# Split attention with a feed-forward network: the score matmuls' operands cut from 128 rows to a head's own 64

## The chip, the cores and the metric

The kernel runs on one core of a Trainium2 chip. The metric is the time of the device in microseconds (us). Two runs of the kernel before took 238.03 and 238.21 us, median 238.12.

The engines are named as the profile names them: PE is TensorE's matmul stream and PEld its weight loads (one operand of a matmul is first loaded into the array as weights, the other then streams through), DVE is VectorE, ACT ScalarE, POOL GpSimd, SP SyncE, which here only issues DMAs. L405 is line 405 of the kernel.

## The reference

Attention over 4 batches, 8 heads, 768 positions and 64 values per head. Heads 0, 2 and 6 see all earlier positions. The other five see the first 4 positions and the last 64. The eight heads' outputs stand side by side as 512 features of 3,072 tokens, which a two-layer network with a leaky rectifier takes from 512 to 2,048 and back to 512.

```python
scores = scale * np.matmul(q, k.transpose(0, 1, 3, 2))
stream_keep = causal & (is_sink | in_win)          # n_sink = 4, window = 64
mask = where(is_retrieval[h], causal, stream_keep)
a = softmax(where(mask, scores, -1e9))
x = (a @ v)  ->  [3072, 512]
h = x @ w_in
out = (max(h, 0) + alpha * min(h, 0)) @ w_out
```

## The kernel before

The work is cut into 16 segments (n = 0 to 15): four batches, and in each four pairs of heads, `PAIRS = [(0, 1), (2, 3), (6, 7), (4, 5)]`. `hh` (0 or 1) is a head's place in its pair. All matmuls take bf16 operands and add up in fp32 in PSUM, which is treated as eight banks of 512 columns.

**Queries and keys.** The score matmul contracts over the 64 values of a head, so queries and keys are needed with these values on the partitions. `qT[n % 4]` holds both heads of a segment one above the other: head 0 on rows 0 to 63, head 1 on rows 64 to 127. The keys have one array for each head, `kTs[n % 4][hh]`, of 128 rows: the head's own 64 rows (64 hh to 64 hh + 63) carry its keys and the other 64 rows are zeros, written at the start by the items kz0 to kz3. A score matmul over all 128 rows thus multiplies the other head's queries by zero. In segments 0 to 7 the transposes are done on TensorE (`to_array`, L342 to L348) and copied out by `put_q` (L353) and `put_k` (L368, L372 to L374). From segment 8 on DMAs transpose (`dma_q`, `dma_k`); the zeros then come along with the transposed rows, from a buffer zeroed by the items nz0 and nz1.

**Scores.** `S_retr` (a head that sees everything) and `S_stream` (a head with a window) write the scores with the keys on the partitions, 128 keys at a time: the keys are the weights and the queries stream. `S_retr` lays six blocks of keys one after another and cuts the whole into six parts of equal length, so that a matmul (L405) has anything from 16 to 488 columns. `S_stream` has 176 or 192 columns per block of keys, fewer at the end (L438 from segment 8 on, L444 before). In segments 0 to 3 a mask is added on TensorE, by a second matmul of the identity with a mask of large negative numbers into the same columns (L408, L447); from segment 4 on masked entries are instead multiplied by zero after the exponential, on VectorE (`M_retr`, `M_stream`). Each score item takes a bank of PSUM, or two before segment 4, which the exponential on ScalarE (L415, L463, L469) gives back.

**What follows.** `AV` (L501) multiplies the exponentials by the values, with a column of ones beside the values for the sums. `AV_out` (L510, L511) divides. The result is transposed to `xT`, on TensorE (L523, L528) or by DMA. `P1` (L543) is the first layer, `relu` and `prelu` (L548 on ScalarE, L555 on VectorE) the rectifier, `P2` (L563) the second layer, L569 and L573 the way out. The slopes alpha are transposed once on TensorE (L593). `warm` (L642) is a row of matmuls that uses nothing, ahead of the first transposes.

**Order.** Nothing is planned while building. `ORDER`, at the head of the file, names every item of work (S5.0.2 is score part 2 of head 0 in segment 5, s5.0.2 its exponential, m5.0.2 its mask, A, X, P and O as above), and the program issues the items in this order; each engine takes its own in that order. Feed-forward items of one batch are laid between score and attention items of the next. The last score matmuls start at 166.5 us; attention, transposes and feed-forward work follow. Instructions wait for each other by semaphores that follow from the tiles, rows and columns they read and write.

Of the kernel before, what the change touches and what calls it, by code (L numbers as in the profile page):

```python
# [73 lines left out]
def kernel(  # L74
# [14 lines left out]
    B, H, S, D = q.shape  # L89
# [31 lines left out]
    def tiles(n):  # L121
        return NEAR if n >= LAY else FAR
# [34 lines left out]
    NF, NK, NV, NR, NS = 4, 4, 5, 2, 3  # L157
# [11 lines left out]
    qT = [qT_all[:, i] for i in range(NK)]  # L169
    kTs = [[kT_all[:, i, h] for h in range(2)] for i in range(NK)]  # L170
# [213 lines left out]
    def score_bank(n, hh, m):  # L384
        held["S", n, hh, m] = got = take(*(SC2 if n < 4 else SC))
        return P[:, got[0]:got[0] + len(got), :]

    def r_parts(n, m):
        return range(2 * m, 2 * m + 2) if n < 4 else [m]

    def S_retr(n, hh, m):
        qt, kt = qT[n % NK], kTs[n % NK][hh]
        QS, RM, RO, RB = tiles(n).QS, tiles(n).RM, tiles(n).RO, tiles(n).RB
        sc = score_bank(n, hh, m)
        for x, part in enumerate(r_parts(n, m)):
            lo, hi = RB[part], RB[part + 1]
            for j in range(6):
                o, w = RO[j], S - QS[j]
                a, z = max(lo, o), min(hi, o + w)
                if a < z:  # L400
                    c = QS[j] + a - o

                    y = min(z, o + RM[j])
                    masked = n < 4 and a < y
                    nc.tensor.matmul(sc[:, x, a - lo:z - lo], kt[:, 128 * j:128 * (j + 1)],  # L405
                                     qt[:, c:c + z - a], start=True, stop=not masked)
                    if masked:
                        nc.tensor.matmul(sc[:, x, a - lo:y - lo], ident, nmr[:, max(j - 1, 0), a - o:y - o],  # L408
                                         start=False, stop=True)
# [19 lines left out]
    def thirds(n, m):  # L429
        return (range(0, 2), range(2, 3))[m] if n < 4 else range(m, m + 1)  # L430

    def S_stream(n, hh, m):
        qt, kt = qT[n % NK], kTs[n % NK][hh]
        sc = score_bank(n, hh, m)
        if n >= LAY:
            for x, j in enumerate(range(2 * m, NT if m == 2 else 2 * m + 2)):
                w = min(176, S - 112 * j)
                nc.tensor.matmul(sc[:, 0, 176 * x:176 * x + w], kt[:, 128 * j:128 * (j + 1)],  # L438
                                 qt[:, 112 * j:112 * j + w], start=True, stop=True)
            return  # L440
        for x, part in enumerate(thirds(n, m)):
            o = 0
            for j, w in THIRD[part]:
                nc.tensor.matmul(sc[:, x, o:o + w], kt[:, 128 * j:128 * (j + 1)],  # L444
                                 qt[:, 124 * j:124 * j + w], start=True, stop=n >= 4)
                if n < 4:
                    nc.tensor.matmul(sc[:, x, o:o + w], ident, (nms6 if j == 6 else nms)[:, 0:w],  # L447
                                     start=False, stop=True)
                o += w
# [247 lines left out]
    for n in range(NSEG):  # L697
# [21 lines left out]
        for hh, h in enumerate(heads(n)):  # L719
            k_ = (3 if n < 4 else 6) if RETR[h] else (2 if n < 4 else 3)  # L720
            for m in range(k_):
                item(f"S{n}.{hh}.{m}", S_retr if RETR[h] else S_stream, n, hh, m)
                item(f"s{n}.{hh}.{m}", E_retr if RETR[h] else E_stream, n, hh, m)
                if n >= 4:
                    item(f"m{n}.{hh}.{m}", M_retr if RETR[h] else M_stream, n, hh, m)
            item(f"A{n}.{hh}", AV, n, hh)
            item(f"a{n}.{hh}", AV_out, n, hh)
# [63 lines left out]
```

## Time and profile before

| | |
|---|---|
| median of the runs | 238.12 us |
| the profiled execution's own time | 237.75 us |
| its span, first to last instruction | 236.0 us |
| TensorE, matmuls (PE) | 226.6 us busy, 1,997 records |
| TensorE, weight loads (PEld) | 143.2 us busy, 2,026 records |
| VectorE | 160.2 us busy |
| ScalarE | 137.1 us busy |
| score matmuls L405, busy | 24.3 us, x132 |
| score matmuls before segment 8 of the heads with a window, L444, busy | 10.4 us, x70 |
| mean granted TensorE clock | 1.000 |

A line of the groups of instructions gives source line, engine, operation, the tile written and the tiles read, the shape and the count; after the bar the busy time in us and the mean length of one in ns. For matmuls the shape begins with the rows and columns of the array that are used (128*128), then partitions x columns of the moving operand. A line of the instructions in order of time gives start and length in us, then the same. In the page's slices each digit is the busy share of one fortieth of the span, in tenths. Matmuls are pipelined: the length of one reaches to the modelled end of its last column, and the next one starts well before that. The chain that ended last is followed back from the last instruction, at each step to what released it.

### The profile page before, as it was taken

To read this page: it belongs to the slowest core of one execution; us is meant where nothing else is said; L and a number is where in the kernel's file an instruction comes from. 1 tells how busy PE (TensorE), PEld (TensorE's weight loads), DVE (VectorE), ACT (ScalarE), POOL (GpSimd) and SP (SyncE) were. 2 spreads that over 40 slices of the span, in tenths; PEclk is the share of its full clock that TensorE was granted. 3 is DMA by queue.
4 is the path that set the end of the run, shared out by engine and by line. 5 is a ranking of instruction groups with operands and counts; after the bars stand their busy time and mean duration, and the time that the engine had idled before them with its cause. 6 is when DMAs were issued, how large, how long until landed. Compare 5 with 4: busy or idle time off the path is not lost.

```text
span 236.0 us, 5222 instructions
## 1 busy us (share of the span) xinstructions
PE 226.6 (96%) x1997; PEld 143.2 (61%) x2026; DVE 160.2 (68%) x404; ACT 137.1 (58%) x265; POOL 45.2 (19%) x92
## 2 busy tenths in 40 slices
PE   7889899999999999999999999999999999999994
PEld 6679555676666644676666455567755554565453
DVE  5879669997998766788994568967961057563020
ACT  6768349988674676785743567858312253650240
POOL 5775884000311800000010010000001010100000
PEclk9999999999999999999999999999999999999999
DMA  6999999998959999998989999961032020010123
GB/s 196 305 247 243 259 247 250 228 204 182 215 89 207 206 240 221 223 156 184 187 174 186 178 244 141 178 95 44 3 68 87 4 89 1 22 71 0 44 102 123
DMA packets 90529, 36.25 MB, mean 154 GB/s; under 512 B 77688, under 2 KB 88712, under 8 KB 90504
## 3 DMA queue, kind: packets, MB, share of 16 engines
q1 hardware_dynamic: 84520, 26.66, 58.4%
q0 software_dynamic: 5664, 8.91, 17.3%
q8 instruction: 16, 0.26, 0.5%
q10 hardware_dynamic: 320, 0.34, 0.4%
q14 instruction: 9, 0.07, 0.1%
HBM read 27.55 MB, written 6.29 MB: 143 GB/s over the span
## 4 chain that ended last, share of the span: by engine, by line
PE 81%; DMA 5%; SPq 4%; DVE 4%; issue 2%; ACT 2%; POOL 0%; POOLq 0%; DVEq 0%; ACTq 0%
PE P L543 33%; PE P L563 31%; PE P L501 6%; PE P L405 4%; DMA vf<-in_v_dram 3%; DMA alpha_r<-in_moe_alpha_dram 2%; PE P L438 2%; PE P L579 1%; SPq L232 1%; DVE g L555 1%; SPq L210 1%; SPq L234 1%; PE P L642 1%; PE P L523 1%; PE P L444 1%
## 5 line engine op out<-in xcount | busy, mean ns | idle before, releaser
L555 DVE SCALAR_TENSOR_TENSOR g<-neg,oma,P 128x256 bf16<-128x256 f32 (+1 forms) x128 | 72.7, 609 | 46.7 <-ACT neg L548 45.5
L543 PE MATMUL P<-xT,w_in_b 128*128 128x256 bf16 (+1 forms) x499 | 92.5, 324 | 0.7
L563 PE MATMUL P<-w_out_b,g 128*128 128x512 bf16 x352 | 86.4, 379 | 0.8
L548 ACT ACTIVATE neg<-P 128x512 f32<-128x512 f32 x96 | 55.0, 606 | 33.5 <-PE P L543 30.3
L543 PEld LDWEIGHTS <-w_in_b 128*128 128x128 bf16 x512 | 48.7, 98 | 29.2 <-issue 0.4
L563 PEld LDWEIGHTS <-g 128*128 128x128 bf16 x368 | 34.0, 98 | 33.4
L415 ACT ACTIVATE eR<-P 128x488 bf16<-128x488 f32 (+4 forms) x63 | 38.0, 624 | 19.2 <-PE P L405 16.6
L573 POOL DMA_DIRECT2D out_dram<-ot x18 | 10.3, 573 | 124.2 <-ACT ot L569 116.6
L569 ACT COPY ot<-P 128x512 f32<-128x512 f32 x23 | 13.2, 589 | 25.1 <-PE P L563 22.7
L405 PE MATMUL P<-qT,kT 128*128 128x280 bf16 (+16 forms) x132 | 24.3, 272 | 0.2
L511 DVE TENSOR_TENSOR xn<-P,rcp 128x448 bf16<-128x448 f32 x32 | 20.0, 624 | 1.1
L463 ACT ACTIVATE eS<-P 128x352 bf16<-128x352 f32 x30 | 14.1, 475 | 8.1 <-PE P L438 8.1
L469 ACT ACTIVATE eS<-P 128x384 bf16<-128x384 f32 (+1 forms) x25 | 13.5, 558 | 5.2 <-PE P L444 2.2
L405 PEld LDWEIGHTS <-kT 128*128 128x128 bf16 x132 | 11.2, 97 | 7.1 <-DVE kT L368 0.2
L501 PE MATMUL P<-vb,eR 128*128 128x65 bf16 x324 | 11.9, 193 | 0.4 <-ACT eR L415 0.3
L501 PEld LDWEIGHTS <-eR 128*128 128x128 bf16 x324 | 11.1, 97 | 1.9 <-ACT eR L415 0.4
L501 PEld LDWEIGHTS <-eS 128*128 128x128 bf16 x260 | 10.3, 97 | 3.0 <-DVE vb L278 0.5
L501 PE MATMUL P<-vb,eS 128*128 128x65 bf16 x260 | 11.1, 193 | 0.3 <-DVE vb L278 0.3
L444 PE MATMUL P<-qT,kT 128*128 128x192 bf16 (+2 forms) x70 | 10.4, 234 | 0.2 <-ACT eR L415 0.2
L478 DVE TENSOR_TENSOR eS<-eS,ms_near 128x352 bf16<-128x352 bf16 x30 | 9.7, 334 | 1.3 <-ACT eS L463 1.3
L333 POOL CAST vb<-vf 128x896 bf16<-128x896 f32 x6 | 5.6, 933 | 25.9 <-DMA vf<-in_v_dram 24.9
L372 DVE COPY kT<-P 64x744 bf16<-64x744 bf16 x9 | 8.4, 933 | 1.6 <-ACT kT L368 1.4
(98 smaller groups left out, 189.7 us busy)
## 6 DMA issues: line engine op xcount, KB each, us to landing
qf<-in_q_dram SPq DMA_DIRECT2D x15, 384.0 KB
out_dram<-ot POOLq DMA_DIRECT2D x18, 256.0 KB, 3.8
vf<-in_v_dram SPq DMA_DIRECT2D x22, 192.0 KB
kf<-in_k_dram SPq DMA_DIRECT2D x21, 192.0 KB
w_in_b<-in_moe_w_in_dram POOLq DMA_DIRECT2D x4, 512.0 KB, 9.6
w_out_b<-in_moe_w_out_dram POOLq DMA_DIRECT2D x4, 512.0 KB, 18.4
kf<-in_k_dram SPq DMA_DIRECT2D x9, 196.0 KB
vf<-in_v_dram SPq DMA_DIRECT2D x9, 196.0 KB
```

Of the source, the lines that this page charges most:

```text
L405: nc.tensor.matmul(sc[:, x, a - lo:z - lo], kt[:, 128 * j:128 * (j + 1)], qt[:, c:c + z - a], start=True, stop=not masked)
L415: nc.scalar.activation(ebuf[n, hh][:, lo:hi].rearrange("p (x c) -> p x c", x=len(parts)), P[:, got[0]:got[0] + len(parts), 0:(hi - lo) // ...
L444: nc.tensor.matmul(sc[:, x, o:o + w], kt[:, 128 * j:128 * (j + 1)], qt[:, 124 * j:124 * j + w], start=True, stop=n >= 4)
L463: nc.scalar.activation(slots, sc[:, 0:352].rearrange("p (s c) -> p s c", c=176), AF.Exp, scale=scale)
L469: nc.scalar.activation(slots, sc.rearrange("p x (s c) -> p x s c", c=192), AF.Exp, scale=scale)
L501: nc.tensor.matmul(pav[:, i, :], e[:, o:o + 128], vv[:, j, hh, 0:D + 1], start=(m == 0), stop=(m == len(terms) - 1))
L511: nc.vector.tensor_tensor(xn[n][:, :, 64 * hh:64 * hh + 64], pav[:, :, 0:D], rcp.to_broadcast([128, NT, D]), op=ALU.mult)
L543: nc.tensor.matmul(psg[:, w * i:w * (i + 1)], w_in_b[:, a, 128 * fb:128 * (fb + 1)], xT[:, c, o:o + w], start=(c == 0), stop=(c == 3))
L548: nc.scalar.activation(neg[t, f], bank(held["P", t, f][0]), AF.Relu, scale=-1.0)
L555: nc.vector.scalar_tensor_tensor(g_buf[t % 2][:, fb, 0:w], neg[t, f][:, c], oma[:, fb:fb + 1], bank(got[0])[:, c], op0=ALU.mult, op1=ALU.add)
L563: nc.tensor.matmul(bank(held["O", t, s][0]), g_buf[t % 2][:, f, 128 * s:128 * (s + 1)], w_out_b[:, f, :], start=(f == 0), stop=(f == 15))
L569: nc.scalar.copy(ot, bank(got[0]))
```

## The change

Both score functions take, of `qT` and of the head's own key array, the 64 rows of that head in place of all 128. For head 0 these are rows 0 to 63, for head 1 rows 64 to 127. The loops over parts and blocks, the columns, the banks and `ORDER` stay. The mask matmuls of segments 0 to 3 still use the identity over 128 rows. The zero rows are still written, though the score matmuls no longer read them.

```diff
     def S_retr(n, hh, m):
-        qt, kt = qT[n % NK], kTs[n % NK][hh]
+        own = slice(D * hh, D * hh + D)
+        qt, kt = qT[n % NK][own], kTs[n % NK][hh][own]
         QS, RM, RO, RB = tiles(n).QS, tiles(n).RM, tiles(n).RO, tiles(n).RB
         sc = score_bank(n, hh, m)
...
     def S_stream(n, hh, m):
-        qt, kt = qT[n % NK], kTs[n % NK][hh]
+        own = slice(D * hh, D * hh + D)
+        qt, kt = qT[n % NK][own], kTs[n % NK][hh][own]
         sc = score_bank(n, hh, m)
```

## The prediction

> **What bounds the kernel now.** I read the views from coarse to fine. First the page: busy times, slices and the shares of the chain that ended last.
>
> ```profile
> PE 226.6 (96%) x1997; PEld 143.2 (61%) x2026; DVE 160.2 (68%) x404; ACT 137.1 (58%) x265; POOL 45.2 (19%) x92
> ...
> PE   7889899999999999999999999999999999999994
> ...
> PEclk9999999999999999999999999999999999999999
> ...
> PE 81%; DMA 5%; SPq 4%; DVE 4%; issue 2%; ACT 2%; POOL 0%; POOLq 0%; DVEq 0%; ACTq 0%
> ```
>
> TensorE is busy in nine tenths of every slice after the first few, at full clock, and it is 81% of the chain. So a nanosecond put into or taken out of its stream moves the end by about as much, wherever no wait of TensorE swallows it.
>
> The busy row counts a matmul to its modelled end, and ends overlap the next start. I therefore go by starts. Two forms in the groups by shape give the rule: 128x65 takes 193 ns, 128x512 takes 379 ns; the slope is 186/447 = 0.416 ns per column, the fixed part 166 ns. In a stream, starts follow each other by the slope alone plus some 2 ns: the 25 attention matmuls from 13.26 us on come about 30 ns apart. Summed that way (columns x 0.416 + 2.4 ns over 1,997 records) TensorE streams 216 us of the 231 between its first and last start. The score matmuls stream 24.4 us of it, in 272 pieces: lines L405 (132), L444 (70), L438 (70).
>
> Then the instructions in order of time, TensorE and its weight loads, in a stretch where all matmuls have one shape of array (128*128):
>
> ```profile
> 6.02 0.35 PE L405 MATMUL P<-qT,kT 128*128 128x454 bf16 x1
> 6.21 0.22 PE L408 MATMUL P<-nmr,ident 128*128 128x128 bf16 x1
> ...
> 6.02 0.10 PEld L408 LDWEIGHTS <-ident 128*128 128x128 bf16 x1
> ```
>
> The weights of the mask matmul L408 load while the score matmul before it streams; 0.19 us after that one's start (454 columns) the next one starts. Nothing is drained.
>
> Last, the two places where the shape of the array changes in this kernel: the transposes of head 0 (L346, 64 columns) give way to full ones (L348), and the 16-row transpose of the slopes (L593) to the feed-forward (L543).
>
> ```profile
> 5.26 0.22 PE L346 MATMUL P<-ident,g 128*64 128x128 bf16 x1
> 5.40 0.11 PEld L348 LDWEIGHTS <-g 128*128 128x128 bf16 x2
> 5.41 0.23 PE L348 MATMUL P<-ident,g 128*128 128x128 bf16 x1
> ...
> 29.69 0.20 PE L593 MATMUL P<-ident_f,alpha_r 16*128 16x16 f32 x1 [1.25 <-DMA alpha_r<-in_moe_alpha_dram]
> 29.83 0.39 PE L543 MATMUL P<-xT,w_in_b 128*128 128x512 bf16 x1
> ...
> 29.82 0.11 PEld L543 LDWEIGHTS <-w_in_b 128*128 128x128 bf16 x2
> ```
>
> Here the next weights do not load under the matmul before. They start 0.07 us before its modelled end, both times: 5.26 + 0.22 = 5.48 against 5.40, 29.69 + 0.20 = 29.89 against 29.82. The next matmul starts with them. L348 waits for a cast of POOL, but that one ended at 5.15 us (0.50 from 4.65), so it isn't the wait.
>
> **What the Trainium skill says.** TensorEngine Tiling (Array Packing), Key Properties: "Changing tiling mode (not just tile) drains the TensorE". The trace agrees at the two places above. TensorE: Matmul & The Clock Gate, Why this matters for your kernels, has a matmul over 32 rows take as long as one over 128; its gain is that matmuls on different rows run side by side. No row of this trace has a half-height array to test it. The same page, What overlaps and what doesn't, lets a weight load overlap a matmul in flight only when the row group differs; L408 above overlaps with the same rows, so for full height the trace decides against it, and for half height it is open.
>
> **The change part by part.**
>
> *Pieces.* Count, columns and order stay, so the 24.4 us of streaming stays: each piece is priced at zero change. From below: pieces of two heads that stand side by side could overlap. By the written order this happens at 8 places from segment 4 on (S5.1.1 with S6.0.4 is one); before that a mask matmul ends every piece or pair. A piece or two of some 80 ns each can hide at each, at most 8 x 0.2 = 1.6 us; I take 0.8. From above: should a weight load not run under the matmul before it when both use the same 64 rows, each of the 272 - 131 = 141 pieces that follow a score piece would wait as at a change of shape, 141 x 105 ns = 14.8 us. I take zero, since L408 and also the 64-column transposes load ahead (starts of L346 reach 56 ns, the 128 columns alone); the 14.8 is kept for the range.
>
> *Changes of shape.* This is the new cost. All other matmuls keep 128 rows, so every unbroken run of score pieces is entered from full height and left to it. Counting runs along TensorE's stream: before segment 4 every run ends at a mask matmul over 128 rows (L408 x18, L447 x35), which makes 53. From segment 4 on there are 99 score items, of which 21 follow another directly: 78 runs. Together 131 runs, 262 changes. Price of one: L346 to L348 has 0.152 us between starts (5.256 and 5.408 in the trace) where streaming takes 0.056, and the next start comes 0.010 later than streaming would have it: 0.106. L593 to L543: its 202 ns less the fixed 166 is 36 ns of streaming, and the next starts came 134 and 360 ns later where 38 and 254 were due: again 0.106. 262 x 0.105 = 27.5 us. Bounds for the unseen change between 128 and 64 rows: zero from below (if half height shares the mode of full height), 0.105 from the nearest rows; I take the upper one, because one of the two rows is a change of rows and the other of columns, and they agree to a nanosecond. A higher price has no row for it.
>
> *What of it lies under waits.* TensorE's waits up to 36 us are few. In starts beyond streaming: 0.72 us at 8.6 (POOL), 0.46 at 12.3 (vb), 0.37 at 14.6 and 0.42 at 16.1 (exponentials), 1.41 at 28.1 (the load of the slopes), and some 0.7 in pieces. The first four, 1.97, go when TensorE comes later: it has 12 changes by 8.6 us and 106 by 26. Of the slopes' load I take 0.5: it is queued on ScalarE at 24.2 us behind exponentials that wait for scores, so it moves along with them. Of the small ones half, 0.35. Hidden: 2.8 us. Bounds: 1.1 (what stands right at a change now) and 7.7 (all the time beyond streaming up to 36 us, the cold start included). After 36 us the excess is 0.2 to 0.8 us in each 12 us, mostly single steps of 0.216, the length of one matmul: lost records, not waits.
>
> *Waits and memory.* The score matmul of head 0 of segment 0 no longer reads the zeroed half (qz0) or its keys' other half. It gains nothing: L405 at 6.02 us waits for ScalarE's copy of q and VectorE's copy of k, which it still needs. The zero fills stay. No wait is added; DMA stays as it is. VectorE (68%) and ScalarE (58%) get scores later, at a lower rate, and have room.
>
> *Sum.* 27.5 - 2.8 - 0.8 = 23.9 us. From the profiled span of 236.0 that gives 259.9; 1.75 us lie around the span (237.75 - 236.0), so 261.65. The median of the runs, 238.12, is 0.37 above the profiled run: **262.0 us**, ten per cent slower.
>
> **Rivals.**
>
> *No drain for half height (not slower).* The mechanism is in the array's control: if 64 rows from 0 or 64 are run as a full array with unused rows, weights load ahead as under L405 now. Price per change then 0 to 0.002 us; the early waits stay, 0.8 may be gained: 237.3 to 238.6, I say 238. It decides below about 0.018 us per change (4.8 us over 262), a sixth of what the two rows show. For it: neither row is a change between 128 and 64 rows in bf16. Against: the 16-row one drained although only rows changed.
>
> *Half the changes drain.* Both rows show a way back to full height; the ways in are covered by waits (for L309's cast and for alpha_r). If only the way out costs: 131 x 0.105 - 2.5 - 0.8 = 10.5, so 249.
>
> *Drain, and no loading ahead inside a run.* 23.9 + 14.8 = 38.7, so 277. For it: the sentence on row groups. Against: the trace at full height.
>
> *Faster by over 2%.* Would need 4.8 us of the 24.4 of score streaming gone, thrice the 1.6 that neighbours on different rows allow; I know no row for it.
>
> **How the numbers follow.** Full drain 0.70 (its own bounds: 27.5 - 7.7 - 1.6 = 18.2 to 27.5 - 1.1 = 26.4, so 256 to 265); half 0.08; none 0.10; drain without loading ahead 0.09; faster 0.03. Range: below, 248 takes in the half case and leaves out 0.13; above, 272 lies between the full case and that without loading ahead, leaving out 0.07. Two per cent, 4.8 us, is about what a measurement of this kernel can tell from no change. Slower: 0.70 + 0.08 + 0.09 = 0.87; same 0.10; faster 0.03.
>
> **What would show it.** The forms of L405, L438 and L444 read 64*128. At each way in and out the next weight load starts 0.07 us before the matmul's modelled end, and the matmul with it. TensorE's busy share stays near 96% all the same, because the drain lies inside the modelled length; its busy time grows to some 250 us. The stretch from the last score to the end (68 us before, from 168 us on) keeps its length; the first 26 us grow by about 8, the middle by about 16. I am wrong if score weights load under a matmul of full height, or if pieces inside a run stand 0.1 us further apart.

## The result and the profile after

The changed kernel takes 261.9 us (261.61 to 262.19 in two runs), 1.0999 times the kernel before, with a 95% interval of 1.0943 to 1.1054. The profiled execution took 262.19 us, its span is 260.4: 24.4 more than before. In the changed kernel line numbers from L405 on are one higher, from L438 on two.

The page after: busy times, slices and shares of the chain.

```profile
PE 252.2 (97%) x1997; PEld 137.7 (53%) x2026; DVE 161.7 (62%) x404; ACT 138.8 (53%) x265; POOL 44.8 (17%) x92
...
PEclk9999979999999999999999999999999999999999
...
PE 92%; DMA 2%; DVE 2%; POOL 1%; issue 1%; ACT 1%; SPq 0%; ACTq 0%; DVEq 0%; POOLq 0%
```

TensorE is even busier by this count, 97%, and 92% of the chain. The added time is not idle time: it lies inside the modelled lengths of the matmuls, where the busy row can't show it. One digit of the clock is new, the 7; it is taken up below.

The instructions in order of time, TensorE and its weight loads, at the first scores:

```profile
6.29 0.36 PE L406 MATMUL P<-qT,kT 64*128 64x454 bf16 x1
6.58 0.23 PE L409 MATMUL P<-nmr,ident 128*128 128x128 bf16 x1
6.74 0.36 PE L406 MATMUL P<-qT,kT 64*128 64x314 bf16 x2
...
6.58 0.10 PEld L409 LDWEIGHTS <-ident 128*128 128x128 bf16 x1 [0.20 <-issue]
6.74 0.11 PEld L406 LDWEIGHTS <-kT 64*128 64x128 bf16 x2
```

The same 454 columns as before are now followed after 0.29 us in place of 0.19. The mask's weights no longer load under the score matmul: they start at 6.58, 0.07 before its modelled end (6.29 + 0.36 = 6.65), and the idle time before them has no releaser. So do the score weights of the next way in, at 6.74 (6.58 + 0.23 = 6.81). But the two score pieces at 6.74 share a shape, and in the trace the weights of the second start at 6.755 us, under the first (the line marked x2 holds both loads): inside a run half height loads ahead as full height does.

Between the starts at all 131 ways in, the median beyond streaming is 0.096 us, at all 131 ways out 0.093, and the next start of the same shape comes 0.010 late.

By stretch: to the start of the last mask matmul of segment 3 25.8 us before and 35.1 after; from there to the start of the last score matmul 140.7 and 155.7; from there to the end 69.5 and 69.6.

### The profile page after: what moved, and what is told of

Its sections match the earlier page's. It is cut to its first block, busy times and chain, and to the rows that moved or that the text cites. A ratio compares the mean times of both kernels' runs of the same rounds, so it can differ in the third digit from the quotient of the medians.

```text
span 260.4 us, 5222 instructions
## 1 busy us (share of the span) xinstructions
PE 252.2 (97%) x1997; PEld 137.7 (53%) x2026; DVE 161.7 (62%) x404; ACT 138.8 (53%) x265; POOL 44.8 (17%) x92
## 3 DMA queue, kind: packets, MB, share of 16 engines
HBM read 27.55 MB, written 6.29 MB: 130 GB/s over the span
## 4 chain that ended last, share of the span: by engine, by line
PE 92%; DMA 2%; DVE 2%; POOL 1%; issue 1%; ACT 1%; SPq 0%; ACTq 0%; DVEq 0%; POOLq 0%
PE P L545 32%; PE P L565 31%; PE P L503 7%; PE P L406 7%; PE P L446 4%; PE P L440 3%; PE P L449 2%; DMA qf<-in_q_dram 2%; PE P L525 2%; PE P L348 2%; PE P L581 1%; PE P L409 1%; DVE ms L607 0%; ACT neg L550 0%; POOL g L318 0%
## 5 line engine op out<-in xcount | busy, mean ns | idle before, releaser
L545 PE MATMUL P<-xT,w_in_b 128*128 128x256 bf16 (+1 forms) x499 | 93.2, 326 | 1.1 <-issue 0.4
L545 PEld LDWEIGHTS <-w_in_b 128*128 128x128 bf16 x512 | 46.6, 98 | 33.9 <-issue 4.8
L565 PEld LDWEIGHTS <-g 128*128 128x128 bf16 x368 | 32.9, 98 | 36.7 <-issue 2.8
L416 ACT ACTIVATE eR<-P 128x488 bf16<-128x488 f32 (+4 forms) x63 | 38.5, 622 | 25.8 <-PE P L406 21.7
L406 PE MATMUL P<-qT,kT 64*128 64x280 bf16 (+16 forms) x132 | 25.7, 274 | 0.1
L465 ACT ACTIVATE eS<-P 128x352 bf16<-128x352 f32 x30 | 14.0, 472 | 11.2 <-PE P L440 11.2
L406 PEld LDWEIGHTS <-kT 64*128 64x128 bf16 x132 | 8.1, 94 | 14.5 <-issue 11.7
L446 PE MATMUL P<-qT,kT 64*128 64x192 bf16 (+2 forms) x70 | 13.3, 241 | 0.0
L512 DVE RECIPROCAL rcp<-P 128x7 f32<-128x7 f32 x32 | 6.4, 200 | 10.2 <-PE P L503 9.9
L503 PEld LDWEIGHTS <-eR 128*128 128x128 bf16 x324 | 10.9, 97 | 1.6 <-issue 0.5
L530 DVE COPY xT<-P 128x768 bf16<-128x768 bf16 x10 | 5.6, 555 | 7.7 <-PE P L525 7.7
```

The source lines that it names most:

```text
L416: nc.scalar.activation(ebuf[n, hh][:, lo:hi].rearrange("p (x c) -> p x c", x=len(parts)), P[:, got[0]:got[0] + len(parts), 0:(hi - lo) // ...
L465: nc.scalar.activation(slots, sc[:, 0:352].rearrange("p (s c) -> p s c", c=176), AF.Exp, scale=scale)
L503: nc.tensor.matmul(pav[:, i, :], e[:, o:o + 128], vv[:, j, hh, 0:D + 1], start=(m == 0), stop=(m == len(terms) - 1))
L545: nc.tensor.matmul(psg[:, w * i:w * (i + 1)], w_in_b[:, a, 128 * fb:128 * (fb + 1)], xT[:, c, o:o + w], start=(c == 0), stop=(c == 3))
L565: nc.tensor.matmul(bank(held["O", t, s][0]), g_buf[t % 2][:, f, 128 * s:128 * (s + 1)], w_out_b[:, f, :], start=(f == 0), stop=(f == 15))
```

## The experiments

The theory, *drain*: time goes with the number of changes between half and full height in TensorE's stream. The rival, *height*: a half-height matmul costs by itself, 23.8 us over 272 pieces, 0.0875 each. Both fit the one result.

**One part at a time: late segments, early segments.**

```diff
-        own = slice(D * hh, D * hh + D)
+        own = slice(D * hh, D * hh + D) if n >= 4 else slice(0, 128)     # late alone
+        own = slice(D * hh, D * hh + D) if n < 4 else slice(0, 128)      # early alone
```

> Segments 0 to 3 read 128 rows again, segments 4 to 15 their own 64. Theory (drain): only the changes of array height cost, 0.106 us each. 156 changes remain: 16.5 us, less 1.4 us for score pieces of two heads that run side by side, hardly anything hidden: 253 us. Rival (height): each half-height piece costs by itself, the 23.8 us of the change over its 272 pieces, 0.0875 us each; 204 pieces: 256 us. The two are close here; the run is to be read with the next one, and it tells how much of the early cost was hidden by waits.

> The other half alone: segments 0 to 3 read their own 64 rows, segments 4 to 15 read 128. Drain: 106 changes, 11.2 us, of which the early waits of TensorE hide 3 to 4 us and a new wait gives back up to 1.3: 245.5 to 247 us. Height: 68 pieces of 0.0875 us: 244 us.

Late alone took 251.69 us (1.0593 times before, 1.0546 to 1.064), early alone 246.79 (1.0358, 1.029 to 1.0427). That is 13.6 and 8.7 us, in sum 22.3 of the 23.8. As they stand, 204 pieces cost less per piece (0.067) than 68 (0.128), while per change it is 0.087 and 0.082.

But the early figure holds a second cost. In three of its four runs the mean granted clock was 0.984 to 0.993, and the drop took 2.9 us of the profiled one (last section). The fourth, at 0.998, took 244.01 us: 5.9 above before, which is what height forecast. Drain, with 11.2 us for the 106 changes, needs what early waits hide: those of the kernel before from 7.5 to 28.1 us, 4.0 us together, are gone from this trace. Late alone, at full clock, came out 1 us under drain's 253 and 4 under height's 256. So this pair leans to drain and doesn't decide.

**More changes, fewer narrow pieces.** Every second piece of an item goes back to 128 rows.

```diff
+        def rows():
+            turn[0] += 1
+            return own if turn[0] % 2 else slice(0, 128)
...
-                    nc.tensor.matmul(sc[:, x, a - lo:z - lo], kt[:, 128 * j:128 * (j + 1)],
-                                     qt[:, c:c + z - a], start=True, stop=not masked)
+                    r_ = rows()
+                    nc.tensor.matmul(sc[:, x, a - lo:z - lo], kf_[r_, 128 * j:128 * (j + 1)],
+                                     qf_[r_, c:c + z - a], start=True, stop=not masked)
```

(The two matmuls of `S_stream` likewise.)

> Only the first, third, fifth piece of each score item reads its own 64 rows, the others 128. 164 half-height pieces instead of 272, but 312 changes of height instead of 262. Drain: 312 x 0.106 = 33.1 us, less some 3 to 4 us under early waits: 267 to 269 us, slower than the changed kernel though fewer pieces are narrow. Height: 164 x 0.0875 = 14.4 us: 252.5 us.

265.5 us (1.1157, 1.1105 to 1.1209): slower than the changed kernel, with 108 fewer narrow pieces and 50 more changes. It is 1.5 us under the range that I gave for drain and 13 above what height forecast. Its four runs had a mean clock of 0.998 to 1.000, those of the changed kernel 0.993 and 0.987, so a lost clock doesn't make it slower. This decides against height. An item of two pieces shows the step. First the changed kernel, then this one, TensorE in order of time (L412 and L558 here are L406 and L545 there; a line marked x2 gives the shape of its first matmul):

```profile
103.21 0.38 PE L406 MATMUL P<-qT,kT 64*128 64x280 bf16 x2
103.52 1.90 PE L545 MATMUL P<-xT,w_in_b 128*128 128x512 bf16 x8
```

```profile
101.26 0.49 PE L412 MATMUL P<-qT,kT 64*128 64x280 bf16 x2
101.59 1.67 PE L558 MATMUL P<-xT,w_in_b 128*128 128x512 bf16 x7
```

The item, 280 and 208 columns, is 0.11 us longer when its second piece has full height: the change has moved into the item. Its way out is then no change, and what follows starts 0.33 us after the item's start, as against 0.31.

**Half height against three quarters.** The first head alone, with 64 rows and with 96. The 32 added rows are zeros in the keys.

```diff
-        own = slice(D * hh, D * hh + D)
+        own = slice(0, 64) if hh == 0 else slice(0, 128)      # 64
+        own = slice(0, 96) if hh == 0 else slice(0, 128)      # 96
```

> Only the first head of each pair reads its 64 rows (0 to 63), the second head reads 128. Drain: 154 changes, 16.3 us, less about 2 us under early waits, no overlap of two heads: 252 to 253 us. Height: 160 pieces, 14 us: 252 us. It serves as the comparison for the run with 96 rows.

> As the run before, but the first head reads rows 0 to 95: its own 64 and 32 rows of zeros in the keys. If any matmul of fewer than 128 rows leaves the array's mode: 252 to 253 us as with 64 rows. If the mode goes by quarters, halves or all of the array, and 96 rows count as all: no drain, 238 us, and weights load under the matmul before at the entries. Height taken as proportional to the rows left out: half of 14 us, 245 us.

With 64 rows 249.32 us (1.0496, 1.0447 to 1.0545), with 96 rows 238.18 (1.0011, 0.9994 to 1.0028). 154 changes to half height cost 11.2 us; as many to 96 rows cost nothing. The trace of the run with 96 rows, at the same scores:

```profile
11.19 0.36 PE L406 MATMUL P<-qT,kT 96*128 96x454 bf16 x1
11.38 0.22 PE L409 MATMUL P<-nmr,ident 128*128 128x128 bf16 x1
...
11.19 0.10 PEld L409 LDWEIGHTS <-ident 128*128 128x128 bf16 x1
```

The mask's weights load under the score matmul, 0.19 us from start to start. So it is not reading fewer rows that drains the array. The Trainium skill, TensorEngine Tiling (Array Packing), Available Configurations, lists arrays of 128, 64 and 32 rows; that 96 rows run as a full one is what this run adds. The run with 64 rows came out 3 us below what I expected: more of it was hidden than the 2 us that I allowed. Its trace no longer has the waits of the kernel before at 12.3, 14.6 and 28.1 us, 2.2 us together, nor some smaller ones.

**Without the mask matmuls.** The masks that cut the runs of segments 0 to 3 are left out, in the changed kernel and in the one before.

```diff
-                    masked = n < 4 and a < y
+                    masked = False
...
-                                 qt[:, 124 * j:124 * j + w], start=True, stop=n >= 4)
-                if n < 4:
-                    nc.tensor.matmul(sc[:, x, o:o + w], ident, (nms6 if j == 6 else nms)[:, 0:w],
-                                     start=False, stop=True)
+                                 qt[:, 124 * j:124 * j + w], start=True, stop=True)
```

> The changed kernel without the 53 mask matmuls of segments 0 to 3, so that the first batch's scores go unmasked into the exponential. This takes out 3.5 us of streaming and joins pieces of a score item into one run: 180 changes instead of 262. Drain: against the changed kernel 3.5 + 82 x 0.103 = 11.9 us less, part of which returns as early waits: 250 to 252 us. Height: 3.5 us less, 258.5 us.

> The kernel before without the same 53 mask matmuls: the control. All matmuls keep 128 rows: 3.5 us of streaming less at most, and waits for loads and exponentials in the first 36 us take some of it back: 235 to 238 us under every theory. The difference to the run without masks at 64 rows should be 180 x 0.106 - 1.4 = 17.7 us (drain, less what early waits hide) or 23.8 us (height).

252.93 us at 64 rows, 237.26 at 128 (0.9971 times before, 0.9938 to 1.0004). Taking out the masks gives 9.0 us at 64 rows, where their streaming is 3.5, and 0.8 at 128. The difference that remains, 15.7 us for 180 changes, is 0.087 each, as with the late segments, and 2.0 less than I expected; height would have left 23.8.

**The new wait.** The changed kernel has a wait of TensorE, from 42.5 to 43.7 us, that was not there before (TensorE in order of time, then VectorE):

```profile
43.72 0.49 PE L348 MATMUL P<-ident,natq 128*128 128x128 bf16 x6 [1.18 <-POOL vb L297]
...
40.34 0.94 DVE L605 TENSOR_SCALAR ms<-nms 128x192 bf16<-128x192 bf16 x2
41.20 1.29 DVE L607 COPY ms<-ms 128x192 bf16<-128x192 bf16 x1
42.42 0.95 DVE L608 COPY ms<-ms 128x148 bf16<-128x148 bf16 x1
...
43.49 0.17 DVE L599 TENSOR_SCALAR oma<-P 128x16 f32<-128x16 f32 x1
```

The profile names GpSimd. But the transposes take a bank of the pair that the slopes' transpose also uses, and that bank comes free with VectorE's copy of the slopes, which ends at 43.66 behind 3 us of mask factors. I moved that copy ahead of them.

```diff
 # ORDER
-P0.4.0 ms wi3 Lk5 ... P0.4.2 al
+P0.4.0 wi3 Lk5 ... P0.4.2 al ms
```

> The changed kernel with one step of VectorE's order moved: the copy of the slopes out of PSUM (al, L599) comes before the mask factors (ms, L605 to L610) instead of after them. If TensorE's 1.2 us wait before the transposes at 43.7 us is for the bank that this copy frees, it goes: 260.5 us. If it is for GpSimd's copy L297, as the list of waits has it, nothing changes: 261.9 us.

261.77 us (1.1001, 1.0921 to 1.1081), where the changed kernel took 261.9. This median can't settle 1.3 us: two of the four runs, at a mean clock of 0.985 and 0.986, took 263.1 us, the other two, at full clock, 260.4 and 260.2. The trace of one with the lower clock shows what became of the wait (lines count 54 lower here, the order list being one line; TensorE, then GpSimd):

```profile
43.80 0.50 PE L294 MATMUL P<-ident,natq 128*128 128x128 bf16 x6
44.13 0.38 PE L491 MATMUL P<-xT,w_in_b 128*128 128x512 bf16 x1
45.64 0.59 PE L491 MATMUL P<-xT,w_in_b 128*128 128x512 bf16 x2 [1.13 <-DVE g L503]
...
44.43 0.34 POOL L243 COPY vb<-vb 4x192 f32<-4x192 f32 x1
```

The wait before the transposes is gone. They start at 43.80, ahead of the GpSimd copy that the profile had named (44.43), so it was the bank. The second feed-forward matmul after them now waits as long for VectorE, which has the mask factors in front of its rectifier instead. The wait belongs to the 3 us of factors, not to one instruction.

**Two heads side by side.** Only seven pairs of items of different heads read 64 rows, and each pair is issued piece by piece in turn.

```diff
+    def pair(x, y):
+        for name in (x, y):
+            paired.append([])
+            I[name]()
+        p, q = paired
+        paired.clear()
+        for i in range(max(len(p), len(q))):
+            for args, kw in p[i:i + 1] + q[i:i + 1]:
+                nc.tensor.matmul(*args, **kw)
...
-        own = slice(D * hh, D * hh + D)
+        own = slice(D * hh, D * hh + D) if paired else slice(0, 128)
```

> All score matmuls read 128 rows except seven pairs of score items of two different heads that already follow each other from segment 5 on; these read their own 64 rows, and their pieces are issued in turn (one of head 0, one of head 1). If pieces on rows 0 to 63 and 64 to 127 run side by side, each pair hides the shorter item, 0.147 to 0.187 us, 1.09 us in all, against 14 changes x 0.106 = 1.48 us: 238.5 us. If they don't run side by side: 239.6 us. The two lie too close for the clock; the starts of the pairs' pieces in the trace decide: equal starts of two heads' pieces, or one after the other.

238.14 us against 237.92 of the kernel before (1.0021, 0.9998 to 1.0043). The pieces do run side by side: in all seven pairs the first two start 3 to 4 ns apart. Items of 176, 176 and of 176, 176, 96 columns start their pieces at 155.944, 155.947, 156.029, 156.033 and 156.109 us. The changed kernel has it too, where two heads happen to meet (TensorE in order of time):

```profile
105.35 0.25 PE L440 MATMUL P<-qT,kT 64*128 64x176 bf16 x1
105.36 0.36 PE L406 MATMUL P<-qT,kT 64*128 64x448 bf16 x1
105.44 0.28 PE L440 MATMUL P<-qT,kT 64*128 64x176 bf16 x2
105.56 0.18 PE L406 MATMUL P<-qT,kT 64*128 64x40 bf16 x1
105.67 0.39 PE L565 MATMUL P<-w_out_b,g 128*128 128x512 bf16 x1
```

448 columns start 10 ns after 176 of the other head. A pair hides its shorter item, 0.147 to 0.187 us; a way in and out costs some 0.2. One pair in a run about breaks even. At best, with one run a segment that takes in all of a segment's scores, the 12 segments from 4 on would hide 0.48 us each (the 1,152 columns of a head with a window) for 0.2: by this estimate 3.3 us, 1.4%. That needs more than the two banks that scores have now, and wasn't tried. No version of the kernel here beats the one before.

## Why the prediction was right

262.0 was forecast and 261.9 measured. The cause and the count of changes were right; that the two figures agree to 0.1 us is luck, since several smaller terms were off and cancelled.

*Bound and method.* Right. TensorE's starts, not its busy time, carried the working. The stretch after the last score kept its length. The early part grew by 9.3 us and the middle by 14.9, where I had about 8 and 16.

*Price of a change.* Forecast 0.106 (0.096 and 0.010 on the next start), from one change of rows and one of columns. Measured 0.096 in and 0.093 out, 0.010 on the next start where there is one. 131 x 0.096 + 131 x 0.093 = 24.8; with 0.010 on the start after each of the 262, another way in or out included (0.106 and 0.103 there), 2.6: 27.4 us, where I had 27.5. The count of 262 was right, and the experiments show that it is the count that matters. Half the changes draining, and no drain at half height, fall by the same rows: both ways drain, alike.

*Loading ahead inside a run.* Taken at no cost, and so it is; the rival with 277 us falls at the second weight load after 6.74 us. Over all 141 pieces that follow a score piece, the time beyond streaming is 1.1 us, neighbours on different rows left aside, where no loading ahead was priced at 14.8.

*Neighbours on different rows.* Taken at 0.8 us of at most 1.6. The starts that come before streaming would allow them sum to 1.4.

*What waits hide.* The step that was sized too small. I took 2.8 us; I had the load of the slopes move along with TensorE. It did move, from issue at 24.2 to 29.8 us, but TensorE reached the slopes at 38.2 instead of 29.7 and didn't wait at all. Of the early waits only 0.28 us, at 9.6, is left. Taking the other terms as measured, 27.4 - 1.4 + 1.2 + 1.3 = 28.5, the span's 24.3 to 24.4 leaves 4.1 to 4.2 hidden.

*What I had not seen.* Two costs are in that sum. The wait above, 1.3 us beyond streaming; I had written that VectorE has room, and judged it by its share of the whole span, not by the 3 us block of mask factors ahead of instructions that TensorE waits for. And a stretch at half clock, 1.2 us, taken up in the last section.

## What to carry to other kernels

In this kernel a matmul over 64 rows streams no faster than one over 128, so cutting zero rows gains nothing by itself, and each step between half height and full height drains the array, here for 0.10 us. Count such steps in TensorE's order before you narrow an operand: zero padding to full height, or to 96 rows as tried here from row 0, costs none of them. By these figures half height pays only in runs long enough that two operands on different rows hide more than one way in and one way out, about 0.2 us; no run here shows a gain.

## What the runs showed that I had not expected

**The clock drops while TensorE is never idle.** A table by stretch of TensorE in the changed kernel (busy us, instructions, granted clock, DMA share, GB/s):

```profile
29.50:32.90 3.40, 3.40 (x31) 1.00 1.25 240
32.90:36.30 3.40, 3.18 (x24) 0.50 1.17 253
36.30:39.70 3.40, 3.35 (x40) 1.00 1.19 240
```

Up to 32.9 us TensorE counts as wholly busy, with a drain at nearly every matmul of segment 3's scores and masks; then the clock is granted at half for 3.413 us. The 23 matmuls in it take 2.95 us from first start to last, where columns and drains at full clock would take 1.79: 1.2 us lost. The run with early segments alone and the one with the slopes' copy moved had 6.827 us at half clock, and lost 2.9 and 3.1. Late segments alone, and every second piece alone, had no drop in their profiles.

The drop comes and goes between runs of one kernel, as with early segments alone. So the 23.8 us of the change aren't all drain: 1.2 us of the profiled run is lost clock and, by an estimate from its mean clock of 0.987, about 3 of the other.

The Trainium skill, TensorE: Matmul & The Clock Gate, Part 1, has a free-running window of 3413 ns after which an idle array is throttled. The lengths agree, one and two windows, and in all five profiles with a drop the time from the first full clock to the drop is a whole number of them (27.307 us, eight, in the changed kernel). But here the array was draining rather than idle: in the 3.4 us ahead of the three drops named so far columns streamed for 0.45 to 0.48 of the time.

That dense draining causes the drop is argued from this, not shown, and it isn't needed for one. The kernel before without its masks, which has no half-height matmul, had a drop in its profiled run (240.39 us, the longest of its twelve). By stretch of TensorE:

```profile
22.80:26.20 3.40, 1.53 (x22) 1.00 1.08 246
26.20:33.10 6.90, 5.31 (x43) 0.51 1.05 211
```

Here waits came ahead of it, with columns streaming for 0.27 of the window. The changed kernel without its masks dropped likewise from 12.0 to 18.8 us, after 0.41. Nor does the share of columns alone set it: the run of pairs had 0.42 in the window from 7.5 to 10.9 us without a drop, and the kernel before 0.47 in its wait for the slopes, which its windows cut in two. What share keeps the clock up stays open.

**The waiter that the profile named was not the one.** Its GpSimd copy ended within 0.05 us of VectorE's copy of the slopes, and moving the latter moved the wait.
